# Softmax turned in 32x32 blocks by VectorE and swapped through DRAM, in a fused windowed attention and gated MLP

## The chip, the cores and the metric

The kernel runs on one core of one Trainium2 chip. A core has a matrix engine (TensorE, PE in the rows), VectorE (DVE), ScalarE (ACT), GpSimd (POOL) and SyncE (SP), which here only issues DMAs. PEld is TensorE's loading of stationary operands. The metric is the device time in microseconds (us) of one launch; it is given as the median of several runs.

## The reference

```python
B, H, S, D = 8, 8, 576, 64                     # q, k, v: float32
scores = (q @ k^T) / sqrt(D) + slope[h] * -(i - j)
scores = where(0 <= i - j < 128, scores, -1e9)
attn   = softmax(scores)                       # row maximum off, exp, over the sum
x      = (attn @ v) as [B, S, 512]             # heads side by side
h      = relu(x @ w_in)                        # w_in: 512 x 1024
conv   = three taps over the tokens of a batch, one weight per column
out    = (h * sigmoid(conv)) @ w_out           # w_out: 1024 x 512
```

## The kernel before

The 4608 tokens form 36 tiles of 128 queries (t) and 18 chunks of 256 tokens, each chunk with 4 steps of two 128-column blocks of the 1024 (s, 72 in all). Most matrix products of the second half split an operand into a high and a low float32r part and are done in three passes (L602 up, L704 down).

Attention of a tile, in two halves u of four heads: `load` brings q and k by DMA; from tile 9 on they come as 32-row blocks and VectorE turns them (`turn`, L338), ScalarE rounds the high part (`qk_hi`, L351), GpSimd takes the low part (`qk_lo`, L358). `scores` fills four PSUM tiles (L377 from tile 9, L421 before). VectorE puts the previous tile's keys under the mask (`place`, L447), adds the bias with the row's extreme (`add_bias`, L465), and ScalarE takes the exponential and the row sum (`exps`, L473). `recips` (L484, L485) makes 1/sum from 4 elements a partition on VectorE; `normal` (L491) multiplies the 128 x 512 half by it on VectorE. `attnT` (L510) turns the half with four TensorE transposes into one PSUM tile `pa`, ScalarE copies it to SBUF (`attn_out`, L518), and GpSimd cuts it into the part of this tile's keys and that of the previous tile's (`select`, L524, L527). `av` (L543) multiplies with v; `x_hi`, `x_lo` (L559, L565) split the result into the ring of x.

A step of the second half is `up` (TensorE, L602), `relu` (ScalarE, L614), `middle` (ScalarE, L620, the middle tap into the single PSUM tile `zp`), four multiply-adds of the outer taps by VectorE (`conv_side`, L635), `tanh` (ScalarE, L642), `gate` (VectorE, L650), `g_hi` (ScalarE, L662), `g_lo` (GpSimd, L670) and `down` (TensorE, L704).

The order is written out by hand in three strings that `emit` reads piece by piece: OPENING (tiles 0 to 7, weights, steps 0 to 9), PERIOD (two tiles and four steps, 14 times from tile 8) and TAIL. A piece is a name with a tile or step offset and the half: S0.0 scores of tile t, MP place, MB bias, X exponential, N normal, T transposes, RL copy, SEL select, AV, TQ/HQ/LQ turn and split of q and k, UH up, HH relu, Z middle, CA/CB the two outer taps, TH, GT, GH, GL, D down, OB store, LD and LV loads. Each engine, SP too, takes its instructions in this order and waits at one until its operands are there and its buffer is free. The PSUM tag `tr` has 5 buffers, which scores (4 at a time), up, av and pa take in turn.

Of the kernel before, what the change touches and what calls it, by code (L numbers as in the profile page):

```python
# [22 lines left out]
def tile_alibi_window_attention_conv_glu(  # L23
# [475 lines left out]

    def normal_act(t, u):  # L500
# [10 lines left out]
        pas[t, u] = ps  # L511

    def attn_out(t, u):
        if t < FIRST:
            rls[t, u] = apool.tile([P, 2, HU, P], F32, name=f"rl{t}_{u}", tag="rl", bufs=4)
        else:
            rls[t, u] = wpool.tile([P, 2, HU, P], F32, name=f"rl{t}_{u}", tag="wst", bufs=NST)
# [224 lines left out]


# [21 lines left out]
    OPENING = """
    LH0.0 QU0.0 LH0.1 LD1 F0 LD2 QU0.1 F4 QV0.0 LD3 CL0 CL4 S0.0 MA0.0.0 QV0.1 S0.1 F1 QU1.0 MA0.0.1 X0.0.0 RP0
    MA0.1.0 QU1.1 QV1.0 I2 S1.0 SG0 F3 QV1.1 MA0.1.1 X0.0.1 MA1.0.1 OB6 I2 S1.1 I2 QU2.1 F5 X0.1.0 X0.1.1 OB4 MA1.0.0
    X1.0.1 X1.0.0 CL1 LD4 LV0 MA1.1.1 MA1.1.0 SH4 NR0 I1 QU2.0 CL3 X1.1.1 QV2.1 X1.1.0 CL5 I1 QU3.1 I1 S2.1 N0.0
    QV2.0 N0.1 QV3.1 T0.1 NR1 F2 I1 QU3.0 F8 LD5 S2.0 MA2.1.0 N1.1 MA2.1.1 LV1 NA1.0 RL0.1 T1.1 X2.1.0 RS1 SEL0.1 RS4
    I2 S3.1 MA2.0.0 LV2 RL1.1 MA2.0.1 T0.0 V0 QV3.0 X2.0.0 RL0.0 SEL1.1 S3.0 RP3 X2.0.1 X2.1.1 SEL0.0 F7 MA3.1.1 F10  # L770
    MA3.0.0 T1.0 QU4.0 F11 NR2 SG1 SG3 RL1.0 MA3.1.0 CL2 QU4.1 SEL1.0 F12 LD6 QV4.0 NA2.0 F6 LV4 S4.0 NA2.1 CL8 AV0
    MA3.0.1 XL1 XF2 QV4.1 V4 XH0 RP5 MA4.0.0 X3.0.0 T2.0 T2.1 RP2 RL2.0 S4.1 RP8 LD7 F9 QU5.1 MA4.0.1 X3.1.0 RL2.1
    X3.0.1 H0 X3.1.1 SEL2.0 P4 SEL2.1 OB5 V3 MA4.1.1 V1 AV1 W4 F13 H3 SG2 X4.1.1 NR3 SG5 AV2 GH0 XH1 CL10 QU5.0 QV5.1
    XH2 V2 UH1.0 XL0 LV3 S5.1 NA3.0 CL7 RS7 LV5 W0 SG8 QV5.0 X4.0.0 T3.0 H1 RL3.0 XL2 UH1.1 X4.0.1 NA3.1 HH1.0 RS10
    UH0.0 HH1.1 LV6 QU6.0 MA4.1.0 HH0.0 S5.0 SG7 T3.1 SG10 QU6.1 CL6 LD8 UH0.1 V5 X4.1.0 QV6.0 V7 RL3.1 V8 CL12
    MA5.1.1 XF0 RP6 MA5.1.0 NR4 XF3 QV6.1 GH3 NA4.0 HH0.1 SG6 SEL3.0 SEL3.1 V6 T4.0 RL4.0 S6.0 MA5.0.0 Z0.0 SEL4.0
    XF5 NA4.1 F16 UH2.0 CV0.0 MA6.0.0 H2 Z0.1 HH2.0 T4.1 RL4.1 S6.1 CV0.1 RS12 CL13 TH0 X5.1.0 MA5.0.1 W2 F15 AV3
    MA6.1.0 X5.0.1 CL9 XH3 LV8 H7 SEL4.1 GT0 AV4 Z1.0 MA6.1.1 CV1.0 RS9 XH4 W1 XL4 Z1.1 CV1.1 F14 X5.0.0 XL3 KH6.0
    TH1 W3 UH3.0 W7 RS13 H5 HH3.0 SG12 KH6.1 X5.1.1 Z2.0 H8 GT1 GL0 UH2.1 UH3.1 SG9 MA6.0.1 H6 HH2.1 XF4 UH4.0 CL11
    V9 KL6.0 NR5 CV2.0 X6.0.1 V10 KL6.1 W6 GL1 GH1 QU7.1 NA5.0 CL16 Z2.1 UH5.0 CV2.1 CL15 X6.1.1 UH4.1 HH3.1 QV7.1  # L780
    NA5.1 W8 TH2 LV7 T5.0 D0 RL5.0 V12 UH5.1 X6.1.0 HH4 GT2 Z3.0 RS16 RS11 W5 T5.1 QU7.0 QM7.1 CL14 LD10 KT6.1 X6.0.0
    SG16 H4 GL2 CV3.0 UH7.0 N6.1 QV7.0 UH6.0 HH5 T6.1 SG13 RL5.1 XF6 Z3.1 N6.0 RS14 SH14 CV3.1 RL6.1 SEL5.1 SG11 TH3
    UH6.1 T6.0 GT3 QM7.0 SEL5.0 KT6.0 GH2 UH7.1 Z4.0 RL6.0 S7.1 SEL6.0 CV4.0 MA7.1.0 Z4.1 CV4.1 H10 SEL6.1 AV5
    MA7.1.1 H12 RS15 V11 TH4 GT4 HH6 V13 Z5.0 LV9 X7.1.1 X7.1.0 XH5 SG15 AV6 V14 H14 S7.0 CV5.0 D1 Z5.1 GH4 D2 GL3
    V15 H9 HH7 LD9 V16 CV5.1 D3 XL5 H16 MA7.0.1 XH6 W16 TH5 Q8 H11 GT5 XL6 Z6.0 CV6.0 UH8.0 UH9.0 Z6.1 X7.0.1 QO8
    MA7.0.0 CV6.1 N7.1 GL4 UH9.1 XF1 TH6 T7.1 OB3 Z7.0 W10 GT6 W9 H13 W11 CV7.0 GH6 W12 GH5 Z7.1 CV7.1 UH8.1 X7.0.0
    HH8 W14 TH7 Z8.0 GL5 W13 GT7 D4 GH7 QL8 D5 RL7.1 LD11 TQ9 GL6 H15 HH9 W15 CV8.0 Z8.1 GL7 D6 D7 CV8.1 N7.0 SEL7.1
    TH8 GT8 Z9.0 T7.0 OB7 GH8 CV9.0 Z9.1 RL7.0 CV9.1 GL8 TH9 GT9 SEL7.0
# [13 lines left out]
    UH2.1 UH2.0 GL0 Z1.1 CV1.1 UH5.0 TH1 HH2 Z2.1 GT1 UH3.0 GL-1 Z2.0 HH3 CV2.0 CV2.1 TH2 Z3.1 OB-2 OB4 GH1 D-1 GL1
    Z3.0 GT2 UH4.1 CV3.0 UH4.0 CV3.1 GH2 D0 HH5.0 TH3 HH4 Z4.0 Z4.1 GT3 D1 UH5.1 GL2 CV4.0 CV4.1 TH4 OB1 GH3 HH5.1
    GL3 Z5.0 GT4 Z5.1 CV5.0 GH4 TH5.0 GT5.0 OB2 D2 D3 CV5.1 TH5.1 GT5.1 OB3 OB-1 GH5.1 GL4 OB0 D4 GL5.1 GH5.0 GL5.0
    D5 OB5
# [36 lines left out]
```

## Time and profile before

| | us |
|---|---|
| median of 3 runs (613.5 to 614.34) | 613.86 |
| the profiled execution | 613.21 |
| its span, first to last instruction | 611.5 |

A row of the profile's page gives busy time of an engine and its share of the span. Groups of instructions have a count, the busy time and the mean duration of one. Matmuls are pipelined, so durations of TensorE overlap: what one costs is read from start to start, or from the chain of waits, which counts no time twice. The core's granted clock was 1.00 in nearly every stretch of the run, which is 2.4 GHz.

### The profile page before, as it was taken

The numbers are of one execution on the slowest core, as the hardware profiler recorded it, in microseconds if no ns is written. First come the engines' busy times: TensorE is split into PE (matmuls) and PEld (weight loads), VectorE is DVE, ScalarE is ACT, GpSimd is POOL, SyncE is SP. The second block draws the span as 40 slices with busy tenths as digits, with TensorE's granted clock in tenths as the row PEclk, the third lists the DMA queues.
The fourth block names the chain that finished last, engine by engine and source line by source line (L and its number), as shares of the span: only waits on it lengthen the run. The fifth ranks groups of instructions, "written<-read, shape, count | busy, mean of one in ns | idle before, by whom it ended". The sixth has DMA issues, their size and how long they took to land.

```text
span 611.5 us, 15429 instructions
## 1 busy us (share of the span) xinstructions
PE 597.1 (98%) x5497; PEld 522.5 (85%) x5497; DVE 508.1 (83%) x1545; ACT 434.1 (71%) x1198; POOL 292.9 (48%) x362
## 2 busy tenths in 40 slices
...
GB/s 224 251 228 187 113 48 92 95 48 98 57 79 29 86 54 71 70 71 71 37 95 65 84 48 90 46 78 52 92 57 81 41 84 3 65 7 1 36 1 69
DMA packets 128160, 47.44 MB, mean 78 GB/s; under 512 B 121276, under 2 KB 121556, under 8 KB 128084
## 3 DMA queue, kind: packets, MB, share of 16 engines
...
## 4 chain that ended last, share of the span: by engine, by line
PE 72%; DVE 19%; ACT 4%; issue 2%; DMA 1%; SPq 1%; POOL 1%; ACTq 0%; DVEq 0%; POOLq 0%
PE o L704 24%; PE p L602 24%; PE av L543 9%; DVE zp L635 6%; PE sc L377 5%; PE pa L510 3%; DVE e L465 3%; DVE sc L447 3%; PE o L694 2%; DVE e L491 2%; DVE st L484 2%; ACT zp L642 1%; PE sc L421 1%; ACT zp L620 1%; SPq L280 1%
## 5 line engine op out<-in xcount | busy, mean ns | idle before, releaser
L635 DVE SCALAR_TENSOR_TENSOR zp<-hh,cw,zp 128x256 f32<-128x256 f32 (+7 forms) x384 | 161.7, 421 | 47.2 <-ACT zp L620 38.0
L602 PE MATMUL p<-ring,wi 128*128 128x256 f32 x1088 | 197.9, 283 | 0.0
L670 POOL TENSOR_TENSOR gl<-z,gh 128x512 fp32r<-128x512 f32 x67 | 86.7, 1294 | 198.7 <-ACT gh L662 146.1
L602 PEld LDWEIGHTS p<-ring,wi 128*128 128x128 f32 x1088 | 168.4, 188 | 3.4 <-issue 0.8
L602 PE MATMUL p<-ring,wl 128*128 128x256 f32 x544 | 152.4, 280 | 0.0
L473 ACT ACTIVATE e<-e,st 128x128 f32<-128x128 f32 x288 | 112.4, 393 | 11.7 <-DVE st L465 11.7
L704 PE MATMUL o<-wo,gh 128*128 128x512 f32 x270 | 110.0, 407 | 0.0
L704 PE MATMUL o<-wo,gl 128*128 128x512 f32 x270 | 107.2, 397 | 0.0
L704 PE MATMUL o<-wl,gh 128*128 128x512 f32 x270 | 105.3, 390 | 0.0
L602 PEld LDWEIGHTS p<-ring,wl 128*128 128x128 f32 x544 | 102.7, 189 | 0.0
L620 ACT ACTIVATE zp<-hh,cw 128x256 f32<-128x256 f32 x144 | 69.2, 480 | 15.5 <-DVE z L650 8.1
L465 DVE CUSTOM_DVE_ANT_0 e<-sc,bias 128x128 f32<-128x128 f32 x288 | 71.9, 288 | 3.4 <-DVE sc L447 0.2
L642 ACT ACTIVATE zp<-zp 128x512 f32<-128x512 f32 (+1 forms) x73 | 42.2, 578 | 45.0 <-DVE zp L635 42.3
L543 PE MATMUL av<-rl,rv 128*64 128x128 f32 x1088 | 64.8, 275 | 4.3 <-ACT rl L518 1.9
L524 POOL TENSOR_SCALAR_AFFINE_SELECT rl<-rl 128x512 f32<-128x512 f32 x64 | 40.9, 640 | 56.7 <-ACT rl L518 56.7
L543 PEld LDWEIGHTS av<-rl,rv 128*64 128x64 f32 x1088 | 59.1, 137 | 8.8 <-ACT rl L518 3.0
L358 POOL TENSOR_TENSOR qkT_low<-blk,qkT 128x1024 fp32r<-128x1024 f32 (+1 forms) x28 | 66.0, 2358 | 0.0
L650 DVE SCALAR_TENSOR_TENSOR z<-zp,hh 128x512 f32<-128x512 f32 (+1 forms) x73 | 48.9, 670 | 20.0 <-ACT zp L642 15.3
L704 PEld LDWEIGHTS o<-wo,gl 128*128 128x128 f32 x270 | 50.5, 187 | 16.2 <-POOL gl L670 5.2
L518 ACT COPY rl<-pa 128x512 f32<-128x512 f32 x72 | 41.7, 579 | 31.9 <-PE pa L510 31.8
L704 PEld LDWEIGHTS o<-wo,gh 128*128 128x128 f32 x270 | 50.7, 188 | 12.2 <-ACT zp L620 1.9
L614 ACT ACTIVATE hh<-p 128x512 f32<-128x512 f32 x67 | 39.4, 588 | 30.5 <-PE p L602 30.5
...
## 6 DMA issues: line engine op xcount, KB each, us to landing
...
wst<-in_moe_w_in_dram SPq DMA_DIRECT2D x8, 512.0 KB, 5.5
wst<-in_moe_w_out_dram SPq DMA_DIRECT2D x8, 512.0 KB, 4.6
...
```

What stands on the lines that cost most here:

```text
L358: eng.tensor_tensor(out=turned_of(qkT_low, s, i), in0=blks[tt][:, i], in1=hi, op=ALU.subtract)
L465: nc.vector.tensor_tensor_reduce(out=e[:, j, :], in0=s_cur[:, g, :], in1=bias[:, u * HU + j, :], scale=-0.125, scalar=FAR, op0=ALU.add, op ...
L473: nc.scalar.activation(out=e[:, j, :], in_=e[:, j, :], func=AF.Exp, bias=st[:, 0, j : j + 1], scale=-1.0, accum_out=st[:, 1, j : j + 1],)
L518: nc.scalar.copy(out=rls[t, u][:, 0], in_=pas.pop((t, u)))
L543: nc.tensor.matmul(ps[a * D : (a + 1) * D, u * NG + g], vraw[tt][:, u * HU + j], rl[:, side, j], start=n == 0, stop=n == len(sides) - 1,)
L602: nc.tensor.matmul(ps, a[:, part], ring[:, i, cc, cols], start=cc == 0 and n == 0, stop=cc == NCC - 1 and n == 2)
L620: nc.scalar.activation(out=zps[s][:, ff, :], in_=hhs[s][:, ff, 1 : 1 + CW], func=AF.Copy, scale=cw[:, 1, f : f + 1])
L635: nc.vector.scalar_tensor_tensor(out=z[:, ff, a:cut], in0=hh[:, ff, a + kk : cut + kk], scalar=cw[:, kk, f : f + 1], in1=z[:, ff, a:cut], ...
L642: nc.scalar.activation(out=zps[s][:, ff], in_=zps[s][:, ff], func=AF.Tanh)
L650: nc.vector.scalar_tensor_tensor(out=zgs[s][:, ff], in0=zps[s][:, ff], scalar=1.0, in1=hhs[s][:, ff, 1 : 1 + CW], op0=ALU.add, op1=ALU.mult,)
L670: nc.gpsimd.tensor_tensor(out=gl, in0=zgs.pop(s), in1=as32(gh), op=ALU.subtract)
L704: nc.tensor.matmul(to, a[:, ff, ms], w[:, part], start=first and n == 0, stop=end and n == 2)
```

## The change

From tile 8 on (FIRST), the pieces T, RL and SEL are gone. The multiply of N runs on GpSimd instead of VectorE (its `recips` stay on VectorE). `turn_e` (TE) lets VectorE turn the 128 x 512 half in 32 x 32 blocks and writes it grouped by key block into `eb`; `write_e` (WE) stores that 512 KB tile in a DRAM scratch with one DMA; `swap_e` (SE) reads it back with four DMAs of 128 KB, each into 32 partitions, in runs of 1 KB, so that keys end up on partitions; `select_e` (CE) makes the two GpSimd selections in two halves of 64 queries. `av` reads its moving operand from that tile, 128 queries in four pieces of 32. Tiles 0 to 7 go on as before. All three order strings are new: OPENING now also holds the scores of tiles 8 to 10 and their softmax in part, PERIOD computes the scores of tiles t+3 and t+4 and AV of t-1 and t.

```diff
     def normal(t, u):
         if t >= EARLY:
             recips(t, u)
         e, st, pss = sms[t, u]
-        nc.vector.tensor_tensor(out=e, in0=e, in1=st[:, 2, :].unsqueeze(2).to_broadcast([P, HU, P]), op=ALU.mult)
+        eng = nc.vector if t < FIRST else nc.gpsimd
+        eng.tensor_tensor(out=e, in0=e, in1=st[:, 2, :].unsqueeze(2).to_broadcast([P, HU, P]), op=ALU.mult)
         es[t, u] = e
...
+    dram = ctx.enter_context(tc.tile_pool(name="dram", bufs=2, space=bass.MemoryType.DRAM))
+    def turn_e(t, u):
...
+            ebs[t] = apool.tile([P, NB, H, BK], F32, name=f"eb{t}", tag="rl", bufs=4)
+        e = es.pop((t, u))
+        nc.vector.transpose(
+            out=ebs[t][:, :, u * HU : (u + 1) * HU].rearrange("p b h c -> p h b c"),
+            in_=e.rearrange("p h (b r) -> p h b r", r=BK),
+        )
+    def write_e(t):
...
+        scrs[t] = dram.tile([P, NB, H * BK], F32, name=f"scr{t}", tag="scr", bufs=3)
+        nc.sync.dma_start(out=scrs[t], in_=ebs.pop(t).rearrange("p b h c -> p b (h c)"))
+    def swap_e(t):
...
+        sides = sides_of[t] = [
+            wpool.tile([P, NB, H, BK], F32, name=f"{x}{t}", tag="wst", bufs=NST)
+            for x in (("rr", "ll") if (t * P) % S else ("rr",))
+        ]
+        of = scrs.pop(t).rearrange("(j r) b f -> b r j f", r=BK)
+        for b in range(NB):
+            nc.sync.dma_start(out=sides[0][b * BK : (b + 1) * BK].rearrange("p j h c -> p j (h c)"), in_=of[b])
+    def select_e(t, n):
...
+        r, *l = [x[:, 2 * n : 2 * n + 2] for x in sides_of[t]]
...
+    def side_of(t, u, side, j):
+        if t < FIRST:
+            return rls[t, u][:, side, j]
+        return sides_of[t][side][:, :, u * HU + j, :]
...
                         nc.tensor.matmul(
                             ps[a * D : (a + 1) * D, u * NG + g],
                             vraw[tt][:, u * HU + j],
-                            rl[:, side, j],
+                            side_of(t, u, side, j),
...
     PERIOD = """
-    UH0.1 UH0.0 S0.0 MP0.0.0 S0.1 MP0.1.0 HH0 MP0.1.1 HQ1 Z0.0 D-2 Z0.1 GH-1 UH1.1 UH1.0 GL-1 MB0.0.0 X0.0.0 MP0.0.1
...
+    D-3 CE0.0 OB-3 UH1.1 UH1.0 WE1 CE0.1 TH-1 GT-1 D-2 HH0 Z0.0 Z0.1 GH-1 GL-1 TQ3 CA0.0 CA0.1 X2.1.1 HQ3 LQ3 CB0.0
+    AV-1 LD5 XH-1 CB0.1 XL-1 N2.1 X2.0.1 AV0 XF-1 TQ4 HH1 X2.0.0 N2.0 D-1 XH0 XL0 XF0 TH0 GT0 GH0 TE2.1 Z1.0 Z1.1
...
```

On TensorE before, at the first transposes of a period (tile 18): `o` is down, `pa` the transposes, `sc` the scores.

```order
L704 MATMUL o_1_4281<-wo,gh_4295 128x512
L704 MATMUL o_1_4281<-wl_1465,gh_4295 128x512
L704 MATMUL o_1_4281<-wo,gl_4296 128x512
L510 MATMUL pa_0_4361<-ident_r,e_0_4269 128x128 x4
L510 MATMUL pa_1_4375<-ident_r,e_1_4272 128x128 x4
L377 MATMUL sc_0_4386<-qkT_1018 128x256
```

And on TensorE now, where a period's first scores follow a down.

```order
L752 MATMUL o_1_4996<-wo,gh_5013 128x512
L752 MATMUL o_1_4996<-wl_1404,gh_5013 128x512
L752 MATMUL o_1_4996<-wo,gl_5014 128x512
L383 MATMUL sc_0_5133<-qkT_1076 128x256
L383 MATMUL sc_1_5134<-qkT_1076 128x256
L383 MATMUL sc_2_5135<-qkT_1076 128x256
```

The eight transposes between down and scores are gone, and no other instruction of TensorE stands in their place.

On VectorE before, at the softmax scaling of tile 18 (`st` holds the row sums, `e` the half, `zp` the taps, `blk` the turned q and k):

```order
L484 TENSOR_SCALAR st18_0_4270<-st18_0_4270 128x4
L485 RECIPROCAL st18_0_4270<-st18_0_4270 128x4
L491 TENSOR_TENSOR e18_0_4269<-e18_0_4269,st18_0_4270 128x512
L484 TENSOR_SCALAR st18_1_4273<-st18_1_4273 128x4
L485 RECIPROCAL st18_1_4273<-st18_1_4273 128x4
L491 TENSOR_TENSOR e18_1_4272<-e18_1_4272,st18_1_4273 128x512
L635 SCALAR_TENSOR_TENSOR zp30_4278<-hh2_131,cw_121,zp30_4278 128x256 x2
L338 STREAM_TRANSPOSE blk_4382<-rqk20_4033 128x4x4x2x32
```

And on VectorE now, at the same tile:

```order
L613 TENSOR_TENSOR ring_126<-av15_4016,ring_126 128x4x128
L490 TENSOR_SCALAR st18_1_3841<-st18_1_3841 128x4
L491 RECIPROCAL st18_1_3841<-st18_1_3841 128x4
L340 STREAM_TRANSPOSE blk_4076<-rqk20_3912 128x4x4x2x32
L490 TENSOR_SCALAR st18_0_3851<-st18_0_3851 128x4
L491 RECIPROCAL st18_0_3851<-st18_0_3851 128x4
L613 TENSOR_TENSOR ring_126<-av16_4059,ring_126 128x4x128
L618 CAST ring_126<-ring_126 128x8
L698 SCALAR_TENSOR_TENSOR z26_4100<-zp26_3996,hh2_133 128x512
L538 STREAM_TRANSPOSE eb18_4105<-e18_1_3840 128x4x4x32
L538 STREAM_TRANSPOSE eb18_4105<-e18_0_3850 128x4x4x32
```

Two multiplies are replaced by two block transposes, which stand some instructions later and wait for GpSimd; the reciprocals stay.

On GpSimd before, around the same tile (`gl` is the gate's low part, `qkT_low` that of q and k, `rl` the selected softmax):

```order
L670 TENSOR_TENSOR gl29_4296<-z29_4188,gh29_4295 128x512
L671 COPY hh1_130<-hh1_130 128x2x2
L358 TENSOR_TENSOR qkT_low_125<-blk_4084,qkT7_1018 128x1024
L527 AFFINE_SELECT rl18_0_4366<-rl18_0_4366 128x512
L527 AFFINE_SELECT rl18_1_4380<-rl18_1_4380 128x512
L670 TENSOR_TENSOR gl30_4463<-z30_4384,gh30_4462 128x512
```

And on GpSimd now:

```order
L718 TENSOR_TENSOR gl25_4000<-z25_3979,gh25_3999 128x512
L719 COPY hh1_132<-hh1_132 128x2x2
L364 TENSOR_TENSOR qkT_low_125<-blk_4004,qkT7_1076 128x1024
L498 TENSOR_TENSOR e18_1_3840<-e18_1_3840,st18_1_3841 128x512
L498 TENSOR_TENSOR e18_0_3850<-e18_0_3850,st18_0_3851 128x512
L718 TENSOR_TENSOR gl26_4103<-z26_4100,gh26_4102 128x512
L719 COPY hh2_133<-hh2_133 128x2x2
L364 TENSOR_TENSOR qkT_low_125<-blk_4076,qkT7_1076 128x1024
L566 AFFINE_SELECT ll17_4112<-rr17_4111 128x512
```

The two multiplies now stand between the low part of q and k and the low part of the gate, on which a down waits.

## Rows read from the trace of the kernel before

**Rows 1.** Page: busy us (share of the span) and instructions of each engine.
```profile
PE 597.1 (98%) x5497; PEld 522.5 (85%) x5497; DVE 508.1 (83%) x1545; ACT 434.1 (71%) x1198; POOL 292.9 (48%) x362
```
**Rows 2.** Stretches: length, busy of PE, PEld, DVE, ACT, POOL, clock, DMA share, GB/s.
```profile
0.00:50.00 50.00, 45.87 (x352) 36.69 (x352) 42.49 (x170) 42.38 (x145) 29.51 (x49) 1.00 0.94 241
50.00:114.50 64.50, 63.90 (x458) 51.87 (x458) 59.11 (x147) 51.93 (x141) 38.36 (x51) 1.00 0.38 94
162.30:547.80 385.50, 381.92 (x3795) 339.73 (x3794) 329.99 (x1018) 272.94 (x745) 185.34 (x213) 1.00 0.25 62
547.80:606.30 58.50, 57.54 (x460) 51.69 (x460) 34.64 (x86) 32.57 (x75) 17.60 (x26) 1.00 0.05 19
```
**Rows 3.** Chain that ended last, in a period: start us, us, what.
```profile
144.68 0.44 PE pa L510 x4
145.12 2.91 PE o L704 x12
148.02 0.44 PE pa L510 x4
148.46 2.86 PE p L602 x24
151.32 1.62 PE sc L377 x42
152.94 2.97 PE o L704 x12
155.91 2.83 PE p L602 x24
158.74 2.75 PE o L704 x12
161.49 0.87 PE pa L510 x8
162.37 1.91 PE sc L377 x38
```
**Rows 4.** Groups by line: out<-in, count | busy us, mean ns | idle before, releasers.
```profile
L518 ACT COPY rl<-pa 128x512 f32<-128x512 f32 x72 | 41.7, 579 | 31.9 <-PE pa L510 31.8
L491 DVE TENSOR_TENSOR e<-e,st 128x512 f32<-128x512 f32 x63 | 47.1, 750 | 2.1
L338 DVE STREAM_TRANSPOSE blk<-rk 128x512 f32<-128x512 f32 x1 | 0.7, 702 | 0.0
L338 DVE STREAM_TRANSPOSE blk<-rqk 128x1024 f32<-128x1024 f32 x27 | 33.5, 1240 | 0.1
L670 POOL TENSOR_TENSOR gl<-z,gh 128x512 fp32r<-128x512 f32 x67 | 86.7, 1294 | 198.7 <-ACT gh L662 146.1 <-DVE zp L635 31.3 <-DVE st L465 14.7
L543 PE MATMUL av<-rl,rv 128*64 128x128 f32 x1088 | 64.8, 275 | 4.3 <-ACT rl L518 1.9 <-DVE st L465 0.9 <-POOL rl L527 0.7
L484 DVE TENSOR_SCALAR st<-st 128x4 f32<-128x4 f32 (+1 forms) x66 | 31.8, 482 | 0.6 <-ACT e L473 0.2
```
**Rows 5.** Timeline, DVE and POOL: start us, us, engine, what.
```profile
314.51 0.43 DVE L447 COPY_PREDICATED sc<-m_prev,sc 128x256 f32<-128x256 uint8 x1
...
315.40 0.48 DVE L635 SCALAR_TENSOR_TENSOR zp<-hh,cw,zp 128x256 f32<-128x256 f32 x1
...
317.14 2.40 POOL L358 TENSOR_TENSOR qkT_low<-blk,qkT 128x1024 fp32r<-128x1024 f32 x1
317.26 2.31 DVE L484 TENSOR_SCALAR st<-st 128x4 f32<-128x4 f32 x1
...
320.43 0.16 DVE L484 TENSOR_SCALAR st<-st 128x4 f32<-128x4 f32 x1
```
**Rows 6.** Waits by engine and line: us in total, times, longest.
```profile
DVE zp L635 <- ACT zp L620: 38.0, 33, 2.2
```
**Rows 7.** DMA issues: KB each, median us to landing.
```profile
wst<-in_moe_w_in_dram SPq DMA_DIRECT2D x8, 512.0 KB, 5.5
rv<-in_v_dram SPq DMA_DIRECT2D x8, 128.0 KB, 3.3
```

More of the change, by code (lines that the diff above doesn't have):

```diff
@@ L335, in turn @@
     def turn(t):
+        if t < TURN:
+            return
         for tt, i in ([((t - 1, "k"), slice(1, 2))] if t == TURN else []) + [(t, slice(0, 2))]:
@@ L348, in qk_hi @@
     def qk_hi(t):
+        if t < TURN:
+            return
         for tt, i in ([((t - 1, "k"), slice(1, 2))] if t == TURN else []) + [(t, slice(0, 2))]:
@@ L351, in qk_hi, with qk_lo @@
             nc.scalar.copy(out=turned_of(qkT_of(t), s, i), in_=blks[tt][:, i])
-    def qk_lo(t, pool=True):
-        eng = nc.gpsimd if pool else nc.vector
+    def qk_lo(t):
+        if t < TURN:
+            return
+        eng = nc.gpsimd
         for tt, i in ([((t - 1, "k"), slice(1, 2))] if t == TURN else []) + [(t, slice(0, 2))]:
@@ L513, in attn_out @@
     def attn_out(t, u):
[L514 to L517, printed above, removed]
+        rls[t, u] = apool.tile([P, 2, HU, P], F32, name=f"rl{t}_{u}", tag="rl", bufs=4)
         nc.scalar.copy(out=rls[t, u][:, 0], in_=pas.pop((t, u)))
@@ L529, in select @@
         )
+    dram = ctx.enter_context(tc.tile_pool(name="dram", bufs=2, space=bass.MemoryType.DRAM))
+    ebs, scrs, sides_of = {}, {}, {}
+    def turn_e(t, u):
+        if t < FIRST:
+            return
+        if t not in ebs:
+            ebs[t] = apool.tile([P, NB, H, BK], F32, name=f"eb{t}", tag="rl", bufs=4)
[5 more added lines that the diff above has]
+    def write_e(t):
+        if t < FIRST:
+            return
+        scrs[t] = dram.tile([P, NB, H * BK], F32, name=f"scr{t}", tag="scr", bufs=3)
+        nc.sync.dma_start(out=scrs[t], in_=ebs.pop(t).rearrange("p b h c -> p b (h c)"))
+    def swap_e(t):
+        if t < FIRST:
+            return
+        sides = sides_of[t] = [
[6 more added lines that the diff above has]
+    def select_e(t, n):
+        if t < FIRST:
+            return
+        r, *l = [x[:, 2 * n : 2 * n + 2] for x in sides_of[t]]
+        q0 = 2 * n * BK
+        if l:
+            nc.gpsimd.affine_select(
+                out=l[0], in_=r, pattern=[[-BK, 2], [0, H], [-1, BK]], compare_op=ALU.is_ge, fill=0.0, base=-1 - q0,
+                channel_multiplier=1,
+            )
+        nc.gpsimd.affine_select(
+            out=r, in_=r, pattern=[[BK, 2], [0, H], [1, BK]], compare_op=ALU.is_ge, fill=0.0, base=q0,
+            channel_multiplier=-1,
+        )
+    def side_of(t, u, side, j):
+        if t < FIRST:
+            return rls[t, u][:, side, j]
+        return sides_of[t][side][:, :, u * HU + j, :]
     def av(t):
@@ L737, in tile_alibi_window_attention_conv_glu @@
     TILE = {
-        "LD": load, "LH": load_half, "QU": qkT, "QV": qkT_out, "LV": loadv, "Q": qk, "QO": qk_out, "QL": qk_rest, "QM": qkT_rest, "TQ": turn, "HQ": qk_hi, "LQ": qk_lo, "MP": place, "MB": add_bias, "KH": keys_hi, "KL": keys_low, "KT": keys_top, "S": scores, "MA": merge,
+        "LD": load, "LH": load_half, "QU": qkT, "QV": qkT_out, "LV": loadv, "Q": qk, "QO": qk_out, "QL": qk_rest, "QM": qkT_rest, "TE": turn_e, "WE": write_e, "SE": swap_e, "CE": select_e, "TQ": turn, "HQ": qk_hi, "LQ": qk_lo, "MP": place, "MB": add_bias, "KH": keys_hi, "KL": keys_low, "KT": keys_top, "S": scores, "MA": merge,
         "X": lambda t, u, h: exps(t, u, range(h, HU, 2)),
-        "NR": recips, "N": normal, "NA": normal_act, "NP": normal_pool, "T": attnT, "RL": attn_out, "SEL": select, "AV": av, "XH": x_hi, "XL": x_lo, "XF": xfin,
+        "NR": recips, "N": normal, "NA": normal_act, "T": attnT, "RL": attn_out, "SEL": select, "AV": av, "XH": x_hi, "XL": x_lo, "XF": xfin,
     }
@@ L771, in tile_alibi_window_attention_conv_glu @@
[L771 to L775, printed above, removed]
@@ new lines, in tile_alibi_window_attention_conv_glu @@
+    QU2.1 F5 X0.1.0 X0.1.1 MP1.0.0 MB1.0.0 X1.0.1 X1.0.0 CL1 LD4 LV0 MP1.1.1 MB1.1.1 MP1.1.0 MB1.1.0 SH4 NR0 I1 QU2.0
+    CL3 X1.1.1 QV2.1 X1.1.0 CL5 I1 QU3.1 I1 S2.1 N0.0 QV2.0 N0.1 QV3.1 T0.1 NR1 F2 I1 QU3.0 F8 LD5 S2.0 MP2.1.0
+    MB2.1.0 N1.1 MP2.1.1 MB2.1.1 LV1 NA1.0 RL0.1 T1.1 X2.1.0 RS1 SEL0.1 RS4 I2 S3.1 MP2.0.0 MB2.0.0 LV2 RL1.1 MP2.0.1
+    MB2.0.1 T0.0 V0 QV3.0 X2.0.0 RL0.0 SEL1.1 S3.0 RP3 X2.0.1 X2.1.1 SEL0.0 F7 MP3.1.1 MB3.1.1 F10 MP3.0.0 MB3.0.0
+    T1.0 QU4.0 F11 NR2 SG1 SG3 RL1.0 MP3.1.0 MB3.1.0 CL2 QU4.1 SEL1.0 F12 LD6 QV4.0 NA2.0 F6 LV4 S4.0 NA2.1 CL8 AV0
@@ new lines, in tile_alibi_window_attention_conv_glu @@
+    S6.0 MP5.0.0 X5.1.1 MB5.0.0 Z0.0 SEL4.0 NA4.1 F16 UH2.0 CA0.0 CB0.0 MP6.0.0 MB6.0.0 H2 Z0.1 HH2.0 T4.1 RL4.1
+    SEL4.1 S6.1 CA0.1 CB0.1 LV8 X5.0.0 RS12 CL9 MP6.0.1 SG12 CL13 TH0 CL11 V10 X5.1.0 MP5.0.1 MB5.0.1 F15 W3 LD10
+    KH6.0 KH6.1 W2 H6 UH3.0 MP6.1.1 LD9 MB6.1.1 Z1.0 GT0 GL0 X5.0.1 H8 H7 W7 UH2.1 H5 AV3 MP6.1.0 MB6.1.0 CA1.0 KL6.0
+    CB1.0 V12 MB6.0.1 Z1.1 CA1.1 CB1.1 AV4 XH3 XH4 UH3.1 XL4 X6.1.1 XL3 QU7.1 X6.0.0 TH1 RS9 XF4 NR5 UH5.0 UH5.1
+    UH4.0 UH4.1 LD11 KL6.1 GT1 W6 Z2.0 CA2.0 HH2.1 KT6.1 QV7.1 SG9 W8 HH3.0 HH3.1 CB2.0 Z2.1 CA2.1 QM7.1 S7.1 CB2.1
@@ new lines, in tile_alibi_window_attention_conv_glu @@
+    NA5.1 RS11 SG11 T5.1 V9 D0 TH2 X6.1.0 GT2 V11 GL2 NA5.0 T5.0 CL14 Z3.0 H12 CA3.0 CB3.0 RL5.1 Z3.1 W5 MP7.1.0
+    MB7.1.0 RS13 SG13 CA3.1 CB3.1 H9 UH7.0 W9 MP7.1.1 MB7.1.1 UH6.0 RL5.0 GL1 N6.1 SEL5.0 SEL5.1 TH3 T6.1 QU7.0 GT3
+    UH7.1 X6.0.1 N6.0 T6.0 HH4 CL15 Z4.0 GL3 CA4.0 CB4.0 HH5 RS14 SH14 CL16 V14 QV7.0 QM7.0 KT6.0 RL6.0 UH6.1 Z4.1
+    HH7 H14 RS16 SG16 H10 CA4.1 CB4.1 TH4 GT4 SEL6.0 V13 LV7 AV5 XH5 X7.1.1 Z5.0 S7.0 RL6.1 D1 SEL6.1 AV6 Q8 X7.1.0
+    CA5.0 CB5.0 XL5 D2 MP7.0.1 RS15 Z5.1 HH6 CA5.1 CB5.1 V16 TH5 GT5 SG15 XH6 V15 D3 GH5 Z6.0 CA6.0 CB6.0 Z6.1 XL6
```

57 lines of the change are left out of this document (23 added, 34 removed).

## The prediction

> **What bounds the kernel now.** First the busy shares: TensorE is busy 98% of the span [rows 1], but its matmuls overlap, so that share alone proves little. Then the chain of waits: over a period it is TensorE's own instructions from end to end, down, transposes, up, scores, with no other engine between them [rows 3]. Then the stretches: from 162.3 to 547.8 us, twelve periods of 32.1 us each, VectorE is busy 330.0 us, 27.5 of each 32.1, so it has 4.6 us of idle a period; ScalarE has 272.9, GpSimd 185.3 [rows 2]. The clock is 1.00 throughout, so nothing is to be won or lost there. The reader should see that an instruction taken off TensorE in the periods shortens them, until VectorE's 27.5 us and the waits it can't avoid are as long as TensorE's work.
>
> **TensorE's part.** Per two tiles the chain holds transposes of 0.44, 0.44 and 0.87 us, 1.75 us [rows 3]. There are 28 tiles from tile 8 on, 14 pairs: 14 x 1.75 = 24.5 us go. What follows transposes is longer too: scores 1.91 against 1.62, down 2.91 against 2.75, up 2.86 against 2.83 [rows 3]: 0.48 a period, 6.7 in all. Down is as long behind scores (2.97), and the scores now follow a down in one place, so part of this belongs to any change of kind of matmul. Bounds 0 and 6.7; I take half, 3.4. The count of the other matmuls stays. `av` reads its moving operand in four pieces of 32: no row shows such a read. Its floor is nothing (the bytes are the same); the other end is half speed, which on 848 of the 1088 matmuls that have 64.8 us [rows 4] would be +50.5. I take nothing, for the turned keys already go into the scores by strided views without a visible price.
>
> **VectorE.** Each of 56 halves loses a multiply of 750 ns and gains a block transpose; the one of this size took 702 ns [rows 4], so -0.05 x 56 = -2.7 us of busy time, -0.2 a period. The new one writes in pieces of 32, as the larger ones do. Its reciprocals stay.
>
> In the opening work is drawn forward. Counted by the orders, up to the end of the opening VectorE has in addition: place and bias of tiles 8 to 10, 12 quarter tiles of 0.89 us (from 314.51 to 315.40 [rows 5]), 10.7 us; four block transposes, 2.8; one turn of q and k, 1.24 [rows 4]; four pairs of sum and reciprocal of some 0.35 (0.16 [rows 5] and about as much again), 1.4. That is 16.1. Before, the opening ends at 114.5 us with 101.6 us of VectorE busy and 12.9 idle [rows 2]: now 117.7 busy, 130.6 with the same idle time. TensorE gets three tiles of scores more (4.9) and an up for a down: 119.5. The first thing that must have VectorE's last bias of the opening is the first `av` of the period, which takes the PSUM buffer of tile 10's first scores. Ahead of it stand a down, an up and a down, 8.3 us, so TensorE arrives at 127.8 and waits 2.8. Bounds: 0 (VectorE idles 3 us less) and 11 (the 8.3 us are held up as well). I take 2.8. It isn't won back: the end, from 547.8 on, is TensorE's (57.5 of 58.5 us [rows 2]), and VectorE's spare time there buys nothing.
>
> In a period VectorE needs 27.3 us of then 30.1, with 2.8 idle instead of 4.6. The idle time that the trace lays to somebody is foremost the taps waiting for ScalarE's middle tap, 38.0 us in the run [rows 6], 2.1 per chunk. That much still fits. If all 4.6 stayed, a period would lose 1.8, 22 over twelve. Bounds 0 and 22; I take 0.25 a period, 3.0, being nearer to the end where the named wait fits.
>
> **GpSimd.** 56 multiplies of two inputs at the price of the gate's low part, 1294 ns [rows 4], are 72.5 us: 365 in all, 62% instead of 48%. The selections have as many elements as before. GpSimd had 198.7 us of waits before the gate's low part, nearly all for others [rows 4], so the multiplies go into idle time; if that cover is gone, a down waits for `gl`.
>
> The price that can hurt is another one. The sum of four elements took 2.31 us while GpSimd ran the low part of q and k, from 0.12 us after that began until it ended, and 0.16 us when GpSimd was idle [rows 5]. The mean of 66 is 482 ns [rows 4]: 66 x 0.32 = 21 us of VectorE's busy time, 1.5 a period, is being held up. Now the multiply of the first half runs on GpSimd as the second half's sum comes up. If holds grow with GpSimd's share, 21 x 62/48 = 27, +6 over the run, 0.4 a period; this is within the 2.8. If every one of the four sums of a period meets a long operation at its start, they lose 2.15 and three times 1.1, 5.5 instead of 1.5. That is a rival below. The Trainium skill, "SBUF — State Buffer", section "Who interferes with whom", explains the rows: VectorE and GpSimd share a pair of ports, an instruction in a two-port mode, `tensor_scalar` among them, takes it as an exclusive lock, and the later one waits for the whole of the other. By that rule the reciprocals' sums are the wrong thing to leave on VectorE when GpSimd gets more to do; by it the sum would lie between the +6 and the rival's price. The trace agrees (2.31 against 0.16 us).
>
> **ScalarE and DMA at nothing.** ScalarE loses 56 copies of 579 ns, 32.4 us [rows 4], but is not the bound. Each tile adds a write of 512 KB and four reads of 128 KB. Such DMAs landed after 5.5 and 3.3 us [rows 7], one after the other 8.8. In the order, a tile's write, read and selection are spread over about a period, so 30 us hide it. SP waits at the write for VectorE's transpose, and the q and k loads queued behind it are needed only a period later. The added 29 MB over some 440 us are 67 GB/s beside 62 GB/s that take a 0.25 share of the DMA engines [rows 2]. The opening's first 50 us, at 0.94, get none of it. If the cover is gone, the selection blocks GpSimd's queue and with it `gl` and a down.
>
> **Sum.** The profiled execution took 613.2 us: -24.5 - 3.4 + 2.8 + 3.0 = -22.1, 591.1. The median is 0.65 above the profiled one, so 592.
>
> **Rivals.**
> - Nothing is lost: all 6.7 of the after-effects go and VectorE keeps up in the opening and the periods: 613.9 - 31.2 = 583. For it: the waits named for VectorE fit. Against: scores follow down, the opening has little slack.
> - The shared access takes most of it: 5.5 us of holds a period, 4.0 more than now, VectorE at 31.3 of 30.1. It then sets the period at 31.3 and some 0.3 of waits, 1.5 x 12 = 18 over the forecast: 610 or so. For it: [rows 5]. Against: the sum behind the low part of q and k comes only after the `av` piece that VectorE waits for, when that operation may be over.
> - Slower: VectorE sets the pace with its waits. Place: the twelve full periods, where a tap waits for ScalarE. If its 4.6 us of idle stay whole, a period stays 32.1, TensorE's gain turns into waits, only the last two periods keep 4, and the opening loses its 11: 613.9 - 4 + 11 = 621. It decides from the point where VectorE's busy and waiting time pass 30.1 us a period, and is slower on balance from about 31.4 on with the full opening loss. For it: 2.8 us are not much for an engine that takes its work in order. Against: ScalarE, on which it waits, has 2.3 us less to do per period.
> - `av` at half speed: about 640. Only the missing row speaks for it.
>
> That the transposes stay is not possible: the orders show 64 instead of 288.
>
> **Chances.** The forecast (584 to 600) 0.58; nothing lost (below 584) 0.15; the holds (600 to 612.6) 0.12; no change, within 0.2%, which is about what a measurement of this kernel can tell, 0.04; slower by VectorE's pace 0.09, by `av` 0.02. So faster 0.85, same 0.04, slower 0.11. The range 579 to 608 leaves out the two upper cases, the top of the holds and a little below.
>
> **What would show it.** Periods (from one even tile's scores to the next) of 30 to 30.5 us and a chain still of TensorE; VectorE busy about 27.3 us in each; block transposes of 0.7 and multiplies on GpSimd of 1.3; the summing instruction's mean near 0.5 us; the first period starting at some 120 to 131 us; `av` of 64 matmuls as now. Wrong: a chain in the periods that runs through VectorE or ScalarE, TensorE's idle time in periods over 1 us each, a mean of the sums over 1 us, selections that wait for a DMA.

## The result and the profile after

The changed kernel takes 590.2 us in the median (589.87 to 590.52) against 613.68 of the kernel before on the same chip: a ratio of 0.9617, 95% interval 0.96 to 0.9634. The forecast was 592. The profiled execution took 590.52 us with a span of 588.8, against 613.21 and 611.5.

The busy shares of the page after, beside [rows 1]:

```profile
PE 572.0 (97%) x5273; PEld 496.5 (84%) x5273; DVE 496.7 (84%) x1545; ACT 401.5 (68%) x1142; POOL 359.7 (61%) x418
```

TensorE has 224 matmuls and 25 us less, GpSimd 67 us more. The stretches, with columns as in [rows 2]: the opening in two parts up to the first down of the periods at 128.2 us, then twelve periods (scores of tile 11 to scores of tile 35), then the end. Between the opening and the twelve periods lie 15.2 us that this table does not have.

```profile
0.00:50.00 50.00, 45.50 (x344) 35.03 (x344) 41.81 (x168) 41.52 (x143) 27.84 (x47) 1.00 0.95 234
50.00:128.20 78.20, 73.64 (x601) 58.35 (x600) 74.18 (x201) 62.70 (x181) 51.17 (x58) 1.00 0.36 93
143.40:505.40 362.00, 357.32 (x3605) 317.68 (x3604) 317.96 (x1015) 244.62 (x696) 239.30 (x259) 1.00 0.52 140
505.40:584.20 78.80, 78.80 (x596) 71.14 (x595) 47.40 (x118) 41.60 (x93) 28.82 (x40) 1.00 0.20 58
```

A period is 30.2 us instead of 32.1. In the second line VectorE is busy 95% of the time and TensorE 94%, where TensorE was busy 63.90 us of 64.50 before [rows 2]: the opening is not TensorE's alone any more. The chain of waits in one period of the changed kernel, to be read beside [rows 3]: first the end of a disturbed period, then an undisturbed one.

```profile
201.68 1.05 DVE st L490
...
204.64 0.59 DVE ring L613
...
205.25 0.60 DVE ring L618
205.85 0.60 DVE z L698
206.48 0.62 ACT gh L710
...
212.20 3.08 PE p L650 x24
215.28 1.62 PE sc L383 x41
216.90 3.04 PE p L650 x24
219.94 2.76 PE o L752 x12
222.70 2.83 PE p L650 x24
225.53 2.75 PE o L752 x12
228.28 3.64 PE av L591 x64
231.93 2.95 PE o L752 x12
234.88 1.13 PE sc L383 x26
```

From 212 us on TensorE follows itself, and at 234.88 us scores stand right behind a down. Before that, VectorE (a sum of four elements, the split of x, the gate) sets the time. What VectorE had just gone through is in the timeline, GpSimd and VectorE together:

```profile
200.30 2.40 POOL L364 TENSOR_TENSOR qkT_low<-blk,qkT 128x1024 fp32r<-128x1024 f32 x1 [0.30 <-ACT qkT L355]
201.60 1.13 DVE L490 TENSOR_SCALAR st<-st 128x4 f32<-128x4 f32 x1
202.76 0.18 DVE L491 RECIPROCAL st<-st 128x4 f32<-128x4 f32 x1
```

The sum of four elements is held until GpSimd's low part of q and k ends at 202.7. Of the twelve periods eight take 28.9 to 29.8 us, the other four 30.9 to 31.9. Into the second of these four the chain comes through DMAs and VectorE's turn of q and k as well:

```profile
302.86 3.73 DMA scr<-eb
...
319.49 2.57 DMA rqk<-in_q_dram
322.09 1.25 DVE blk L340
```

Over the whole span SyncE's queue and DMAs have a larger part of the chain than before. The first line is of the kernel before, the second of the changed one:

```profile
PE 72%; DVE 19%; ACT 4%; issue 2%; DMA 1%; SPq 1%; POOL 1%; ACTq 0%; DVEq 0%; POOLq 0%
PE 49%; DVE 27%; SPq 7%; DMA 6%; ACT 5%; issue 3%; POOL 3%; DVEq 0%; ACTq 0%; POOLq 0%
```

The groups that answer to [rows 4]:

```profile
L498 POOL TENSOR_TENSOR e<-e,st 128x512 f32<-128x512 f32 x56 | 58.2, 1040 | 34.3 <-DVE st L491 30.3 <-ACT e L479 1.1 <-ACT zp L690 0.7
L538 DVE STREAM_TRANSPOSE eb<-e 128x512 f32<-128x512 f32 x56 | 37.8, 692 | 0.9 <-POOL e L498 0.9
L490 DVE TENSOR_SCALAR st<-st 128x4 f32<-128x4 f32 (+1 forms) x66 | 21.8, 331 | 1.6 <-ACT e L479 1.5
L591 PE MATMUL av<-rr,rv 128*64 128x128 f32 x448 | 42.4, 276 | 0.0
L566 POOL TENSOR_SCALAR_AFFINE_SELECT ll<-rr 128x512 f32<-128x512 f32 x50 | 36.1, 722 | 25.2 <-DMA rr<-scr 25.1
```

The block transposes cost what was taken for them, the multiplies on GpSimd less (1040 ns against 1294), `av` with its operand in four pieces takes 3.64 us for 64 matmuls and no more per matmul than before (276 ns against 275). The selections wait for the exchange, 25.1 us here and 12.7 in the other selection line.

### The profile page after: what moved, and what is told of

It reads as the page before. It is cut to its first block, busy times and chain, and to the rows that moved or that the text cites. A ratio compares the mean times of both kernels' runs of the same rounds, so it can differ in the third digit from the quotient of the medians.

```text
span 588.8 us, 15341 instructions
## 1 busy us (share of the span) xinstructions
PE 572.0 (97%) x5273; PEld 496.5 (84%) x5273; DVE 496.7 (84%) x1545; ACT 401.5 (68%) x1142; POOL 359.7 (61%) x418
## 4 chain that ended last, share of the span: by engine, by line
PE 49%; DVE 27%; SPq 7%; DMA 6%; ACT 5%; issue 3%; POOL 3%; DVEq 0%; ACTq 0%; POOLq 0%
PE p L650 20%; PE o L752 17%; DVE zp L683 8%; PE av L591 6%; DVE sc L453 5%; DVE e L471 4%; SPq L280 3%; PE sc L383 3%; DVE z L698 2%; DVE blk L340 2%; DMA scr<-eb 2%; ACT zp L668 2%; DMA wst<-in_moe_w_in_dram 1%; DMA rqk<-in_q_dram 1%; DVE ring L613 1%
## 5 line engine op out<-in xcount | busy, mean ns | idle before, releaser
L650 PE MATMUL p<-ring,wi 128*128 128x256 f32 x1088 | 199.9, 284 | 4.3 <-DVE st L471 1.7
L683 DVE SCALAR_TENSOR_TENSOR zp<-hh,cw,zp 128x256 f32<-128x256 f32 (+7 forms) x384 | 160.9, 419 | 31.9 <-ACT zp L668 22.9
L752 PE MATMUL o<-wo,gh 128*128 128x512 f32 x270 | 107.8, 399 | 0.0
L752 PE MATMUL o<-wo,gl 128*128 128x512 f32 x270 | 105.7, 392 | 0.0
L498 POOL TENSOR_TENSOR e<-e,st 128x512 f32<-128x512 f32 x56 | 58.2, 1040 | 34.3 <-DVE st L491 30.3
L471 DVE CUSTOM_DVE_ANT_0 e<-sc,bias 128x128 f32<-128x128 f32 x288 | 70.3, 285 | 3.4 <-ACT e L479 0.2
L710 ACT CAST gh<-z 128x512 fp32r<-128x512 f32 (+1 forms) x69 | 41.7, 606 | 39.3 <-DVE z L698 39.3
L453 DVE COPY_PREDICATED sc<-m_prev,sc 128x256 f32<-128x256 uint8 x128 | 53.2, 422 | 8.1 <-PE sc L383 7.4
L752 PEld LDWEIGHTS o<-wl,gh 128*128 128x128 f32 x270 | 50.7, 188 | 8.5
```

Source lines behind the costliest of these rows:

```text
L453: nc.vector.copy_predicated(out=s_cur, mask=mask.unsqueeze(1).to_broadcast(shp), data=data)
L471: nc.vector.tensor_tensor_reduce(out=e[:, j, :], in0=s_cur[:, g, :], in1=bias[:, u * HU + j, :], scale=-0.125, scalar=FAR, op0=ALU.add, op ...
L498: eng.tensor_tensor(out=e, in0=e, in1=st[:, 2, :].unsqueeze(2).to_broadcast([P, HU, P]), op=ALU.mult)
L650: nc.tensor.matmul(ps, a[:, part], ring[:, i, cc, cols], start=cc == 0 and n == 0, stop=cc == NCC - 1 and n == 2)
L683: nc.vector.scalar_tensor_tensor(out=z[:, ff, a:cut], in0=hh[:, ff, a + kk : cut + kk], scalar=cw[:, kk, f : f + 1], in1=z[:, ff, a:cut], ...
L752: nc.tensor.matmul(to, a[:, ff, ms], w[:, part], start=first and n == 0, stop=end and n == 2)
```

## Experiments

Each is an edit of the changed kernel unless said otherwise; ratios are to the kernel before, with 95% intervals.

**Transposes added as dead weight (e3).**

```diff
         e = es.pop((t, u))
+        extra = pst.tile([P, HU, P], F32, name=f"xt{t}_{u}", tag="tr")
+        for j in range(HU):
+            nc.tensor.transpose(extra[:, j, :], bias[:, j, :], ident)
```

> The changed kernel with the 224 TensorE transposes put back as dead weight: four transposes of a constant tile into a PSUM tile at each block transpose, with no reader and no wait on the softmax. Theory (what the change gains is TensorE's time, and in the periods the whole of it, 1.75 us per two tiles plus 0.45 of slower neighbours): 590.2 + 24.5 + 6.3 = 621; without the neighbours 615. Rival (the new orders brought the gain, or VectorE sets the pace in the periods, so that the dead weight hides in TensorE's waits): 590 to 605.

Measured: 615.96 us, 1.0024 (1.0009 to 1.0039). Against 0.9617 that is 4.07% of 614, 25.0 us. So taking the transposes out is the gain; with them beside everything else that changed, the kernel is about where it was (0.24% slower). The twelve periods take 31.75 us each, 1.6 more than without. In an undisturbed period the chain shows what they cost:

```profile
209.18 2.94 PE o L755 x12
212.12 0.87 PE xt L540 x8
213.00 1.61 PE sc L383 x37
214.61 3.04 PE p L653 x24
```

0.87 us for eight, as before. The 31 us of the fullest expectation were not reached: over the twelve periods 19.0 us come back, less than the 21.0 of the transposes alone; two of the four periods that VectorE delayed hardly change (31.9 to 31.8 and 31.6 to 31.8 us). That the total is so near 24.5 is partly luck. The scores of tile 11 come at 149.7 instead of 143.4 us, 6.3 later, and this is not only TensorE's work: at 128.9 us two groups of transposes wait 2.1 us for PSUM buffers that scores hold, and for 3.4 us from 131.0 on the granted clock is 0.5 (1.2 GHz), where the two groups take 1.1 us each instead of 0.44.

**The scaling back on VectorE (e1).**

```diff
-        eng = nc.vector if t < FIRST else nc.gpsimd
+        eng = nc.vector
```

> One part undone: the multiply of the softmax halves from tile 8 on goes back to VectorE, all else as in the changed kernel (590.2 us). Theory (VectorE is close to the bound in the periods: 318.0 us busy of 362.0 in twelve periods, 26.5 of 30.2): four multiplies of 0.75 us put 3.0 us more on it, 29.5 of 30.2 before any wait; with 1.5 to 2 us of waits that can't go a period becomes some 31.3, and the whole 603 to 609. Rival (VectorE has room, TensorE alone sets the pace): 590 to 593. A second rival, that taking GpSimd's load away frees the reciprocals' sums from being held and pays for it: at or below 590.

Measured: 620.6 us, 1.0093 (1.0074 to 1.0112): 30 us more than with GpSimd, twice what was expected. Periods take 32.5 us. Not only are 56 multiplies on VectorE again; there some of them and of the sums are held while GpSimd works, 786 and 504 ns in the mean. VectorE has no room for 3 us a period. Four waits of TensorE of over 2 us were each followed by 3.4 us at a granted clock of 0.5, which is part of the 30 us. Without the move to GpSimd the whole change would have been slower than before.

**No sum ahead of the reciprocal (e2).** The row sum is at least 1, so adding 1e-9 in float32 changes nothing.

```diff
-        nc.vector.tensor_scalar(out=st[:, 2, :], in0=st[:, 1, :], scalar1=1e-9, scalar2=None, op0=ALU.add)
-        nc.vector.reciprocal(out=st[:, 2, :], in_=st[:, 2, :])
+        nc.vector.reciprocal(out=st[:, 2, :], in_=st[:, 1, :])
```

> The reciprocals without the sum before them: 1e-9 is no longer added to the row sum, which is at least 1, so the float32 value is the same; the reciprocal reads the row sum directly. It takes away the instruction that VectorE was seen to lose time in while GpSimd runs (331 ns in the mean of 66, 21.8 us in the changed kernel). Theory (holds delay VectorE and so the heavier periods of 31 to 32 us; VectorE sets part of the opening): VectorE is 20 us shorter, the periods come down by about 0.3 each and the opening by 1 to 2, the whole 584 to 588. Rival (VectorE's busy time is not on the path): 590 within 0.7. Rival (the reciprocal is held instead): 590, with a mean of the reciprocals of 300 ns or more instead of 180.

Measured: 584.43 us, 0.9515 (0.9498 to 0.9533), 1.0% under the changed kernel and the best of all. The stretch of the twelve periods, with columns as in [rows 2]:

```profile
140.50:497.20 356.70, 355.79 (x3601) 317.67 (x3600) 301.69 (x963) 244.88 (x696) 237.75 (x259) 1.00 0.52 142
```

The group of the reciprocal, with columns as in [rows 4]:

```profile
L490 DVE RECIPROCAL st<-st 128x4 f32<-128x4 f32 (+1 forms) x66 | 11.3, 171 | 2.7 <-ACT e L479 1.9
```

VectorE has 16 us less to do than in the same stretch of the changed kernel, TensorE is busy 99.7%, a period takes 29.7 us and the longest 30.3. The reciprocal in the sum's place is not held (171 ns). The scores of tile 9 come at 113.3 us instead of 115.9. The edit takes away the sum and its holds together; no run separates the two.

**The same in the kernel before (e11).** The same edit there.

> The kernel before the change, with the sum ahead of the reciprocals taken out in the same way (there 482 ns in the mean of 66, 31.8 us). Theory (there TensorE sets the periods, 32.1 us against some 31.8 of its own work, and VectorE has 4.6 us of idle in each): only some 0.2 a period and 1 to 2 in the opening come back, 608 to 612, ratio 0.991 to 0.997. Rival (VectorE's holds cost the kernel before as much as the changed one, 1% or more): ratio 0.990 or less. Rival (nothing): 0.999 to 1.001.

Measured: 609.77 us, 0.9926 (0.9912 to 0.9941). Periods of 31.9 instead of 32.1, as expected of a kernel that TensorE binds; the opening gave nothing (scores of tile 11 at 162.6 instead of 162.3 us). But the holds did not go away here. The multiply behind the reciprocal, which stays on VectorE in this kernel, takes them over, 1024 ns in the mean instead of 750 [rows 4]:

```profile
L490 DVE TENSOR_TENSOR e<-e,st 128x512 f32<-128x512 f32 x63 | 64.4, 1024 | 2.1
```

One takes 2.60 us from 157.69 on, while GpSimd's low part of q and k runs from 157.34 to 159.74. So of the 31.8 us of the sums 17.3 come back as longer multiplies, and this run can't tell what the holds cost the kernel before.

**No masks for tiles 8 to 10 (e4).**

```diff
+        if FIRST <= t < FIRST + 3:
+            return
         negb = neg.unsqueeze(2).to_broadcast(shp)
```

> Leaves out the predicated copies (previous keys, masks) of tiles 8, 9 and 10, which all stand in the opening: 12 instructions of 0.42 us and one kind of mask on tile 9, some 4 to 5 us less of VectorE there. Theory (the opening is bound by VectorE, 74.2 us busy of the 78.2 from 50 us to the first down of the periods): the first period starts 4 us earlier and the whole takes 586 to 587. Rival (the opening is held by TensorE, the weights' DMAs or GpSimd): 590 within 0.7.

Measured: 590.13 us, 0.9605 (0.9586 to 0.9623), no difference that can be told. The scores of tile 9 come at 114.1, 1.9 us earlier, about the four instructions of tile 8 that stand before them; those of tile 11 2.0 earlier. So what is taken from VectorE ahead of tile 9's scores counts, and what stands behind them does not: from there TensorE is busy without a gap (27.0 of 27.0 us from 113 to 140 us in the changed kernel). The 2 us are gone again by the end: two of the later periods were longer, which I can't explain.

**Plain loads of q and k (e6).**

```diff
-                load_blocks(t, raws[t][:, i], src)
+                fetch(t, raws[t][:, i].rearrange("p g m d -> p (g m) d"), src)
```

> Leaves out the block order of the q and k loads from tile 9 on: each comes by one DMA of 256 KB in its natural layout (two where a batch ends) instead of 8 of 32 KB; VectorE turns the wrong pairs, all work is otherwise the same. SP then issues some 17 to 20 DMAs a period instead of 47. Theory (SyncE's queue, at 0.47 us an issue, holds the loads of tiles 9 and 10 in the opening, and in the periods runs near its limit, 22 us of issuing and the waits for the scratch's write): S of tile 9 starts 4 to 6 us earlier than at 115.9, the whole 583 to 587. Rival (VectorE alone holds the opening and the periods): 590 within 1.

Measured: 588.44 us, 0.9576 (0.9561 to 0.9592). The scores of tile 9 come at 115.3 us, 0.7 earlier, not 4 to 6. The loads do not hold the opening; in the profiled execution the twelve periods are 2.7 us shorter (359.3 instead of 362.0).

**More DMA traffic (e5), and the same with plain loads (e8).**

```diff
+        dup = dram.tile([P, NB, H * BK], F32, name=f"dup{t}", tag="dup", bufs=3)
+        nc.sync.dma_start(out=dup, in_=scr)
```

> Adds load to the DMA queue: behind each tile's four reads the same 512 KB are copied from the scratch to another place in DRAM, 28 times, which nobody reads. Theory (the exchange is hidden; its waits, 38 us on GpSimd before the selections, are GpSimd's spare time): 590 within 1. Rival (the exchange's landing is on the path: selections that come late hold up the gate's low part behind them on GpSimd): 593 to 600, with the waits of the selections for the DMA well over 38 us.

> The plain loads of the kernel above (the block order of q and k left out) together with the 28 unread copies of 512 KB that made the changed kernel 627 us. Theory (the copies cost so much because SP, which takes its queue in order, has no room left for their issue and for longer landings): with two thirds of its issues gone the copies are nearly free, 584 to 594. Rival (the DMA engines or DRAM are the limit): 610 or more, near the 627 of before.

Measured: e5 627.5 us, 1.0216 (1.0175 to 1.0257), far over both expectations; e8, with the same copies, 587.3 us, 0.9553 (0.9539 to 0.9568). e5 has 91.50 MB in 149218 packets, e8 91.44 MB in 142382 at a higher rate, 156 against 147 GB/s. So neither the DMA engines nor DRAM are the limit, but SyncE's queue, which has 772 issues in e5 and 345 in e8. Its timeline in e5 (start us, us, what, count):

```profile
301.65 6.43 SPq L280 DMA_DIRECT2D rqk<-in_k_dram  x12
308.18 0.85 SPq L772 DMA_DIRECT2D out_dram<-ob  x2
309.12 0.40 SPq L547 DMA_DIRECT2D scr<-eb  x1
309.57 2.63 SPq L280 DMA_DIRECT2D rqk<-in_q_dram  x4
```

Issue follows issue, most of them about 0.47 us apart whatever the size (32 KB a load, 512 KB the write), and the scratch's write stands among the loads. SyncE's largest wait there, and GpSimd's wait before one line of the selections:

```profile
SPq L559 <- DMA scr<-eb: 70.4, 16, 6.3
POOL ll L569 <- DMA rr<-scr: 61.3, 17, 7.0
```

In the changed kernel they are 43.3 and 25.1 us. Not all of the 37 us is queueing: after waits of TensorE the granted clock was 0.5 in stretches of 23.9 us together.

**Loads ahead of the second read (e7).** LD6 moves from the end of PERIOD to before SE2.

```diff
-    X3.1.0 MP4.1.1 N3.1 CA3.1 CB3.0 SE2 X3.0.1 ...
+    X3.1.0 MP4.1.1 N3.1 CA3.1 CB3.0 LD6 SE2 X3.0.1 ...
```

> Order alone: in each period the q and k loads of the tile after next (LD6) stand ahead of the second read of the scratch (SE2) instead of at the period's end, so that SP has something to issue while the write lands. Theory (SP's waits for the scratch, 43 us in the run, delay what is queued behind them): that wait falls under 15 us, time 587 to 590. Rival (the queue has room in the undisturbed kernel): 590 within 0.7. It is slower than 591 if the selections then come too late.

Measured: 599.88 us, 0.9761 (0.9746 to 0.9777), 9 us slower than the changed kernel. SP's wait for the write falls to 12.6 us as expected, but two periods take 34.3 and 35.7. TensorE's longest wait:

```profile
PE av L591 <- POOL rr L570: 8.6, 3, 4.5
```

The second read of a period is now issued 9 to 11 us after its write in most periods, where it was about 4, and the selections come too late. The exchange is hidden in the changed kernel, but not by much.

**Two attempts to go on from e2 (e9, e10, e12).** Both edits stand on top of e2's: in e9 the scaling of tiles 6 and 7 goes to GpSimd too, in e10 ScalarE issues the output stores, and e12 has both.

```diff
-        eng = nc.vector if t < FIRST else nc.gpsimd
+        eng = nc.vector if t < EARLY else nc.gpsimd
...
-            nc.sync.dma_start(out=out_flat[g0 : g0 + P, :], in_=ob)
+            nc.scalar.dma_start(out=out_flat[g0 : g0 + P, :], in_=ob)
```

> On top of the kernel without the sum (0.9515 of before): the softmax scaling of tiles 6 and 7, four multiplies of 0.75 us, goes from VectorE to GpSimd as well. Theory (all that the opening loses it loses to VectorE before the scores of tile 9): those come 1.5 to 3 us earlier than at 113.3 us, ratio 0.947 to 0.949. Rival (the way over GpSimd makes the transposes of tiles 6 and 7 late, or GpSimd's weights are held up): 0.951 to 0.955.

> On top of the kernel without the sum: the stores of the output are issued by ScalarE, which made the data, instead of SyncE. SP then never waits for ScalarE's copies (69 us in the changed kernel) with the scratch's DMAs queued behind. Theory (SP's queue has little room, and the selections' waits for the exchange follow from it): those waits fall from some 52 us, ratio 0.948 to 0.951. Rival (in the undisturbed kernel SP's waits are room): 0.9515 within 0.0015. Slower if 35 issues of some 0.45 us on ScalarE are on the path.

> The three edits together: no sum, scaling of tiles 6 and 7 on GpSimd, stores issued by ScalarE. If both single edits gain, their gains add, 0.944 to 0.948; if one of them loses, this shows the sum of the two as well.

Measured: 0.9575 (0.9551 to 0.9599), 0.9689 (0.967 to 0.9707), 0.9786 (0.9764 to 0.9809): 587.82, 595.72 and 602.3 us, all worse than 0.9515. In e9 TensorE waits for the early transposes' halves from GpSimd, up to 2.0 us at once, and tile 9's scores come at 117.9 instead of 113.3 us; one stretch of 3.4 us there has the granted clock at 0.5 (1.2 GHz). e12 loses a little more than e9 and e10 together, which would be 0.975. In e10 ScalarE stands at its store's turn until loads that SyncE issued have landed, and TensorE waits for its copies:

```profile
ACT ob L767 <- DMA rqk<-in_k_dram: 18.5, 5, 7.2
PE o L751 <- ACT ob L767: 7.6, 3, 4.0
```

## Why the prediction was right, step by step

The forecast's mechanism held: TensorE's transposes went, nothing else took the whole of it back. That the forecast of 592 is within 2 us is in part luck: the opening lost 5.5 us more than forecast, and what comes behind it gained 6.1 us more.

- **The transposes, 24.5.** Put back as dead weight they cost 25.0 us (e3), of which a part is a wait and a slower clock in the opening; in the twelve periods they cost 19.0 us for 21.0 of their own time.
- **Slower neighbours, 3.4.** An undisturbed period takes 29.7 instead of 31.9 us, both with TensorE alone in the chain: 2.2 us, where the transposes account for 1.75. The other 0.45 is nearly the whole 0.48 of the neighbours, 6.3 us over 14 periods. The step that failed is the half taken for them.
- **VectorE in the periods, 3.0.** The twelve periods take 362.0 instead of 385.5 us. 23.5 are gained where transposes and neighbours together would give 12 x 2.23 = 26.8, so 3.3 are lost, 0.27 a period against the 0.25 taken. Four periods lose 1.1 to 2.2 us each; the kernel before had waits too, 3.6 us of TensorE idle in the twelve [rows 2].
- **Outside the twelve periods, nothing forecast.** From the end of the opening (114.5 us before, 128.2 after) to the end of the span 497.0 us became 460.6. 5.4 of that are three tiles of scores, an up and four transposes of tile 7, less a down, that had moved into the opening; 31.0 are gained, 7.5 of them outside the twelve periods, where two periods' share would be 4.5. Of the 3.0 left over, 2.4 is time in which TensorE was idle before, 1.5 us in the stretch below and 1.0 in the end (57.54 of 58.50 [rows 2]); the changed kernel has none there (15.20 of 15.20 us from 128.2 to 143.4, 78.80 of 78.80 in the end). The line of the kernel before, with columns as in [rows 2]:

```profile
114.50:162.30 47.80, 46.33 (x430) 41.22 (x429) 40.98 (x126) 33.65 (x93) 22.12 (x24) 1.00 0.30 77
```

- **The opening, 2.8.** TensorE reaches the first down of the periods at 128.2 us. The 119.5 worked out left out the four transposes of tile 7, 0.4, so TensorE is 8.3 us late; the bound was 11. The place was wrong: it does not wait at the first `av`, which follows its down at once, but before the scores of tile 9. Between 50 and 113 us it is busy 58.44 of 63.00 us, 4.6 idle, where the kernel before has 0.6 idle in the whole of its stretch; the other half of the 8.3 is not idle time in the trace, and its cause is open. VectorE's busy time was right (116.0 by 128.2 us against 117.7 by the sum), yet the sum placed the meeting of the two engines at the end and gave TensorE 8.3 us of room (a down, an up and a down) that it does not have. e2 and e4 move tile 9's scores by about what they take from VectorE ahead of them; e6 shows that it is not the loads. That VectorE's extra work alone makes the 8.3 was not tried.
- **The multiply on GpSimd.** 1040 ns instead of 1294. The holds did not grow with GpSimd's share, as the +6 supposed; they fell to some 66 x (331 - 160) = 11 us. In e1, with less work on GpSimd than in the changed kernel, the sums' mean is higher (504 ns), so the share does not set it; that it is what the sums meet in the order is not shown. The sum is on the path nevertheless: taking the instruction away gave 6 us (e2). The rival of the holds named the right instruction, but its condition, that holds grow, did not come. The rule in the Trainium skill's "SBUF — State Buffer", section "Who interferes with whom", on the ports that VectorE and GpSimd share is borne out again, by `tensor_scalar` at 1.13 us under a running GpSimd instruction. The reciprocal was not held in any run here (205 ns at most).
- **VectorE's pace (the slower rival)** did not come, but e1 shows how near it was: 3 us a period more on VectorE and the kernel is slower than before. Two of the forecast's signs of being wrong did show, a chain through VectorE (in four periods of twelve) and selections that wait for a DMA (25.1 and 12.7 us), without the time going with them: TensorE is idle 4.7 us in twelve periods.
- **DMA at nothing.** Nearly right in the result (plain loads gain some 2 us, e6): the write landed after 3.7 us, a read after 2.9, estimated 5.5 and 3.3. But the cover that the text named, a period of TensorE's time, was not what counted. The cover is the room in SyncE's queue, which issues some 47 DMAs a period at 0.45 us and waits in between (e5, e7, e8).
